# An S4 kernel generator: the fine magnitudes straight from the exponential, one product of 512 in place of one of 1024

## The chip, the cores and the metric

The kernel runs on one core of a Trainium2 chip. Its time is the device time of one execution in microseconds; smaller is better. Five engines run side by side, each with its own queue that it works off in order: PE (TensorE, matrix products), DVE (VectorE, elementwise), ACT (ScalarE, functions from tables, copies), POOL (GpSimd) and SP (SyncE, which here issues most transfers).

## The reference

A block of a network with two halves, over a sequence of 2048 positions and 512 channels. The first half is a diagonal state-space layer (S4): each channel has 128 complex states, and its convolution kernel K is a sum of 128 complex exponentials. The second half is a dense layer of 512 to 1792, Mish, and 1792 to 512. Cut to what matters:

```python
dt = exp(log_dt)[:, None]
logdA = dt * (A_re + 1j * A_im)             # 512 channels x 128 states
dB = dt * (B_re + 1j * B_im)
P = exp(logdA[:, :, None] * arange(2048))   # a power for each position
K = einsum("dn,dnl,dn->dl", C, P, dB).real  # 512 x 2048
y = irfft(rfft(pad(h)) * rfft(pad(K)))[:2048] + h * Dskip   # h: normalised, modulated input
x = x + ga * y
h = layernorm(x) * (1 + cb) + sb
x = x + gb * (mish(h @ w1 + b1) @ w2)
```

The diff concerns the generation of P and K.

## The kernel before, in words

A position l is written as 64 i + j, with i from 0 to 31 (coarse steps) and j from 0 to 63 (fine steps). The power at l is the product of a coarse power, exp(64 i logdA), and a fine one, exp(j logdA), which also carries the constant of the state (B, C and dt). So K for a channel is a product of two matrices over the 128 states: 32 coarse columns on one side, 64 fine columns on the other, once for the real parts and once for the imaginary ones. PE makes these products (`s_kgen`, L347, tile pkg).

The 512 channels go in 32 steps k of 16 channels. A coarse or fine power is a magnitude (a real exponential) times a cosine or a sine, and these come in two ways:

- **Angles.** PE makes the angles of 32 coarse and 32 fine columns (`s_ang`, L312, tile pang), ACT takes the absolute value and two sines (`s_sin`, L321) into a tile ec of 2 x 16 x 96 numbers a partition, with columns 0 to 31 coarse, 64 to 95 fine and 32 to 63 free. Only 32 fine angles are made, symmetric about the middle: the other 32 fine columns have the same angles with the sign turned, so the same cosines and the sines negated.
- **Magnitudes.** PE multiplies the logarithms of the magnitudes by constants (`mc`, made at L61 and L66), NM = 48 numbers a channel: 32 coarse steps, 8 steps of eight fine positions, 8 single fine positions. ACT takes the exponential of the product (`coarse`, L302, tiles pco and co), in two halves of 8 channels, so 384 numbers a partition and instruction. For the fine magnitudes, DVE multiplies the 8 by the 8 to 64 (`s_mag`, L329, tile m, 1024 numbers).

`comb` (L335) is the work of DVE that puts both together, four multiplies: the lower half of the fine columns (read from columns 95 down to 64, written to 32 to 63), the upper half's first plane, the same for the second plane with the sign turned, and the coarse columns. Then PE can make pkg. ACT copies it to SBUF (`s_ks`, L356, tile ks); DVE adds the direct term Dskip to four of its columns (`s_skip`, L360); PE transforms the coarse axis (`s_ka`, L363, tile pka), and ACT copies that to the large tile gk (`s_tm`, L371).

**The order.** The sines and the exponentials are in different tables of ACT, so the exponentials of 8 steps are made together in a `visit` (L581): table change, 16 pairs of product and exponential through two PSUM buffers, table change back. Visit 0 stands ahead of step 0, visits 1 to 3 behind steps 7, 15 and 23. The order of DVE, ACT and PE is written out by hand and forced. In step k, PE does pkg(k-1), pang(k+3), pka(k-3) and then other work; ACT does ks(k-1), other work, the sines of k+2 and the copy for k-3; DVE does `own`, the list made of comb(k), s_mag(k+1) and s_skip(k-2), with further work of the step spread between its entries (`extra`): parameters of later channels (`params`), the input's layer norm (`u_stats`, `u_norm`). Some of that other work on PE and ACT is the transform of the normalised input (`u_mm`, tile pua, and `u_out`); its result goes to memory. At the end of steps 7, 15 and 23, s_mag(k+1) comes behind the visit instead.

The tile ec has three buffers, so the sines of step k+3 need pkg(k) done; pang's PSUM has two buffers; co has nine and m two. Behind the generation stands the convolution itself in the frequency domain (`product`, `inverse`), and then the second half with its dense products (`mm1`, `mm2`).

## Time and profile before

| | us |
|---|---|
| median of three runs | 737.81 (733.92 to 740.18) |
| profiled execution | 739.76 |
| its span, first to last instruction | 738.0 |
| busy: PE, DVE, ACT | 644.8, 430.2, 317.6 |
| generation, with its start | 0 to about 276 |
| convolution and the dense half's start | about 276 to 390 |
| dense half | about 390 to 738 |

In the profile, a tile is named without its buffer's number, and groups of instructions by what they write and read: `ec<-ec,m` is a multiply of comb, `ec<-ec,co` its last one, `m<-co` is s_mag, `co<-pco` the exponential, `ks<-ks,dtap` is s_skip. Nearly all instructions go through a helper, so their lines are those of the helper (L119, L141, L147). A number in brackets behind an instruction is the time its engine sat idle before it, with what ended that. The granted clock is the share of its full clock that PE was given.

### The profile page before, as it was taken

The numbers are of one execution on the slowest core, as the hardware profiler recorded it, in microseconds if no ns is written. First come the engines' busy times: TensorE is split into PE (matmuls) and PEld (weight loads), VectorE is DVE, ScalarE is ACT, GpSimd is POOL, SyncE is SP. The second block draws the span as 40 slices with busy tenths as digits, with TensorE's granted clock in tenths as the row PEclk, the third lists the DMA queues.
The fourth block names the chain that finished last, engine by engine and source line by source line (L and its number), as shares of the span: only waits on it lengthen the run. The fifth ranks groups of instructions, "written<-read, shape, count | busy, mean of one in ns | idle before, by whom it ended". The sixth has DMA issues, their size and how long they took to land.

```text
span 738.0 us, 11828 instructions
## 1 busy us (share of the span) xinstructions
PE 644.8 (87%) x4848; PEld 438.9 (59%) x4848; DVE 430.2 (58%) x813; ACT 317.6 (43%) x466; POOL 5.0 (1%) x12
## 2 busy tenths in 40 slices
PE   0388889769889988999826999999999999999996
PEld 0246647546655752333205877887788877888884
DVE  8789989998978756876539224431424424441113
ACT  2466587677876953453305322322123222322220
POOL 2000000000000000000000000000000000000000
PEclk9969868997985999999976999999999999999998
DMA  6741023522323258996286522022400500011002
GB/s 184 270 147 49 30 81 107 187 87 80 137 87 115 88 172 239 301 298 205 85 204 183 127 58 57 1 50 64 104 11 1 115 0 1 1 34 25 0 1 57
DMA packets 34314, 74.56 MB, mean 101 GB/s; under 512 B 5418, under 2 KB 9902, under 8 KB 33748
## 3 DMA queue, kind: packets, MB, share of 16 engines
q1 hardware_dynamic: 33380, 72.17, 33.6%
q10 hardware_dynamic: 576, 1.05, 0.7%
q8 instruction: 38, 0.62, 0.3%
q0 software_dynamic: 304, 0.59, 0.3%
q14 instruction: 16, 0.13, 0.1%
HBM read 49.66 MB, written 24.13 MB: 100 GB/s over the span
## 4 chain that ended last, share of the span: by engine, by line
PE 72%; DVE 15%; ACT 6%; DMA 4%; issue 2%; SPq 0%; DVEq 0%; ACTq 0%
PE pm L798 22%; PE po L815 21%; PE pang L147 5%; DVE ec L119 4%; PE pub L147 4%; PE pz L147 4%; PE pkb L147 3%; PE pkg L147 3%; PE pka L147 3%; PE pco L147 3%; PE pua L147 2%; PE pia L763 2%; DVE raw L119 2%; DVE m L119 2%; ACT ec L141 1%
## 5 line engine op out<-in xcount | busy, mean ns | idle before, releaser
L798 PE MATMUL pm<-hh,w1h 128*128 128x512 f32 x448 | 143.3, 400 | 0.6 <-ACT hh L119 0.6
L141 ACT ACTIVATE mh<-pm,b 128x512 f32<-128x512 f32 x56 | 38.5, 688 | 229.3 <-PE pm L798 229.3
L119 DVE TENSOR_TENSOR mal<-mh,mah 128x512 fp32r<-128x512 f32 x56 | 38.7, 691 | 156.4 <-ACT mah L119 156.0
L798 PEld LDWEIGHTS pm<-hh,w1h 128*128 128x128 f32 x448 | 85.3, 190 | 21.8 <-ACT hh L119 1.5
L815 PE MATMUL po<-w2h,mah 128*128 128x512 f32 x224 | 89.5, 400 | 0.0
L798 PE MATMUL pm<-hh,w1l 128*128 128x512 f32 x224 | 89.3, 399 | 0.0
L815 PE MATMUL po<-w2l,mah 128*128 128x512 f32 x224 | 88.6, 396 | 0.0
L815 PE MATMUL po<-w2h,mal 128*128 128x512 f32 x224 | 88.6, 395 | 0.0
L147 PE MATMUL pang<-ac,s 96*128 96x512 f32 x128 | 55.1, 476 | 26.8 <-DMA s<-pkd 26.8
L119 DVE TENSOR_TENSOR ec<-ec,m 128x1024 f32<-128x1024 f32 x64 | 61.0, 954 | 9.1 <-ACT ec L141 8.6
L147 PEld LDWEIGHTS pkg<-ec 128*32 128x32 f32 x2048 | 36.2, 117 | 35.6 <-issue 29.5
L147 PE MATMUL pkg<-ec 128*32 128x64 f32 x2048 | 41.1, 236 | 14.3 <-DVE ec L119 11.5
L119 DVE TENSOR_TENSOR y<-pkb,f 128x1024 f32<-128x1024 f32 x32 | 37.7, 1220 | 25.3 <-PE pkb L147 25.3
L815 PEld LDWEIGHTS po<-w2h,mah 128*128 128x128 f32 x224 | 42.2, 188 | 14.6 <-ACT mah L119 4.9
L147 PEld LDWEIGHTS pang<-ac,s 96*128 96x128 f32 x128 | 28.6, 224 | 34.3 <-issue 27.6
L147 PE MATMUL pco<-mc,s 64*128 64x384 f32 x64 | 33.6, 603 | 17.6 <-ACT co L141 17.2
L798 PEld LDWEIGHTS pm<-hh,w1l 128*128 128x128 f32 x224 | 42.7, 191 | 10.1
L815 PEld LDWEIGHTS po<-w2h,mal 128*128 128x128 f32 x224 | 42.1, 188 | 10.1
L815 PEld LDWEIGHTS po<-w2l,mah 128*128 128x128 f32 x224 | 42.1, 188 | 9.7
L147 PE MATMUL pang<-am,s 96*128 96x512 f32 x128 | 44.9, 437 | 0.0
L119 DVE TENSOR_TENSOR m<-co 128x1024 f32<-128x1024 f32 x32 | 39.0, 1219 | 8.5 <-ACT co L141 8.5
L119 DVE TENSOR_TENSOR ec<-ec,co 128x1024 f32<-128x1024 f32 x32 | 39.1, 1221 | 0.0
(97 smaller groups left out, 867.8 us busy)
## 6 DMA issues: line engine op xcount, KB each, us to landing
ud<-u SPq DMA_DIRECT2D x16, 512.0 KB, 3.1
ur<-ud SPq DMA_DIRECT2D x32, 256.0 KB, 4.5
zd<-z SPq DMA_DIRECT2D x16, 512.0 KB, 2.9
zl<-zd SPq DMA_DIRECT2D x28, 256.0 KB, 4.9
x<-in_A_u SPq DMA_DIRECT2D x32, 128.0 KB, 2.9
x<-in_A_u SPq DMA_DIRECT2D x8, 512.0 KB, 6.7
out<-ot SPq DMA_DIRECT2D x32, 128.0 KB, 2.2
w1s<-in_B_w SPq DMA_DIRECT2D x8, 448.0 KB, 6.8
```

The source lines that it names most:

```text
L119: ins = getattr(self.engine, name)(*a, **kw)
L141: follow("act", nc.scalar.activation(out, in_, f, **kw))
L147: follow("pe", T.matmul(out, lhsT, rhs, start=start, stop=stop))
L763: T.matmul(p[64 * tl:64 * tl + 64, :], di, ZL[tt, hv][:, j % 2, tl, :], start=True, stop=True)
L798: T.matmul(p, w1[wi][:, k, fs], hh[:, hi, k, :], start=(n == 0), stop=(n == 3 * KB - 1))
L815: T.matmul(PO[tt][q], a[ai][:, P * q:P * q + P], w2[wi][:, f, :], start=(f == 0 and n == 0), stop=(f == FB - 1 and n == 2))
```

## The change

NM goes from 48 to 64: the constants are now one column for the factor 32, 31 coarse steps (1 to 31; step 0 has magnitude 1), and all of the first 32 fine steps, with the state's constant in these. So the coarse products and their exponentials grow from 384 to 512 columns. s_mag multiplies the 32 fine magnitudes by that of 32 steps, 512 numbers, to get the upper half; m has one buffer instead of two. comb's first multiply reads the lower magnitudes from co; its last one leaves column 0 out (31 columns of 32). In `own`, s_skip moves from the end to behind the first multiply, and s_mag from there to the end. The tile gs (gains of the input's modulation) moves to a pool that is closed at step 26.

```diff
-NM = 48
+NM = 64
...
-    fac = np.concatenate([64 * np.arange(32), 8 * np.arange(8), np.arange(8)])
+    fac = np.concatenate([[32], 64 * np.arange(1, 32), np.arange(32)])
...
-            mc[4 * d + part, d] = fac if part < 2 else np.arange(NM) < 32
+            mc[4 * d + part, d] = fac if part < 2 else np.arange(NM) >= 32
...
     def s_mag(k):
-        m = M2[k] = gen.tile([P, 16, 64], F32, tag="m2", name=f"m2_{k}", bufs=2)
-        V.tensor_mul(m.rearrange("p d (a b) -> p d a b", a=8),
-                     CO[k][:, :, 32:40, None].to_broadcast([P, 16, 8, 8]),
-                     CO[k][:, :, None, 40:48].to_broadcast([P, 16, 8, 8]))
+        M2[k] = gen.tile([P, 16, 32], F32, tag="m2", name=f"m2_{k}", bufs=1)
+        V.tensor_mul(M2[k], CO[k][:, :, 32:64], CO[k][:, :, 0:1].to_broadcast([P, 16, 32]))
 
     def comb(k):
         ec, m = EC[k], M2[k]
         v = Later()
-        v.tensor_mul(ec[:, :, :, 32:64], ec[:, :, :, 95:63:-1], m[:, None, :, 0:32].to_broadcast([P, 2, 16, 32]))
-        v.tensor_mul(ec[:, 0, :, 64:96], ec[:, 0, :, 64:96], m[:, :, 32:64])
-        v.scalar_tensor_tensor(ec[:, 1, :, 64:96], ec[:, 1, :, 64:96], -1.0, m[:, :, 32:64],
-                               op0=OP.mult, op1=OP.mult)
-        v.tensor_mul(ec[:, :, :, 0:32], ec[:, :, :, 0:32], CO[k][:, None, :, 0:32].to_broadcast([P, 2, 16, 32]))
+        v.tensor_mul(ec[:, :, :, 32:64], ec[:, :, :, 95:63:-1], CO[k][:, None, :, 32:64].to_broadcast([P, 2, 16, 32]))
+        v.tensor_mul(ec[:, 0, :, 64:96], ec[:, 0, :, 64:96], m)
+        v.scalar_tensor_tensor(ec[:, 1, :, 64:96], ec[:, 1, :, 64:96], -1.0, m, op0=OP.mult, op1=OP.mult)
+        v.tensor_mul(ec[:, :, :, 1:32], ec[:, :, :, 1:32], CO[k][:, None, :, 1:32].to_broadcast([P, 2, 16, 31]))
         return v.ops
...
-        g = conv.tile([P, 2, D], F32, name="gs")
+        g = pre.tile([P, 2, D], F32, name="gs")
...
         own = comb(k) if 0 < k < NG else []
+        own.insert(1, lambda: step(s_skip, k - 2))
         if k % 8 != 7:
-            own.insert(1, lambda: step(s_mag, k + 1))
-        own.append(lambda: step(s_skip, k - 2))
+            own.append(lambda: step(s_mag, k + 1))
```

## The prediction

> **What bounds the kernel now.** I read the page first, then busy times by stage, the groups of VectorE (DVE) and ScalarE (ACT), and last the order of time around the waits. The page's clock row:

> ```profile
> PEclk9969868997985999999976999999999999999998
> ```

> One slice is 18.5 us. Nearly all dips (to 5 to 8 tenths) lie between 20 and 276 us, where the kernel is generated: 32 steps k, and four visits in which ACT changes tables and makes the coarse exponentials. The diff's instructions all lie there. By stage (columns: us, then busy PE, PEld, DVE, ACT, POOL, then granted clock; after visit 0, the rows of 11 us hold the visits):

> ```profile
> 43.00:97.00 54.00, 47.19 (x642) 32.55 (x641) 52.25 (x92) 35.57 (x51) 0.00 (x0) 0.83 0.22 75
> 97.00:108.00 11.00, 9.36 (x45) 4.66 (x47) 8.75 (x19) 9.00 (x18) 0.00 (x0) 0.59 0.00 0
> 108.00:161.00 53.00, 44.72 (x711) 31.60 (x702) 51.46 (x102) 38.01 (x57) 0.00 (x0) 0.89 0.43 141
> 161.00:172.00 11.00, 9.12 (x72) 5.10 (x76) 10.23 (x13) 9.27 (x18) 0.00 (x0) 0.63 0.00 0
> 172.00:220.00 48.00, 43.32 (x683) 30.02 (x674) 41.06 (x70) 36.83 (x54) 0.00 (x0) 0.91 0.35 117
> 220.00:231.00 11.00, 8.63 (x69) 5.21 (x73) 9.31 (x11) 8.51 (x18) 0.00 (x0) 0.59 0.05 7
> 231.00:276.00 45.00, 43.06 (x796) 29.48 (x790) 29.05 (x40) 31.03 (x46) 0.00 (x0) 0.91 0.44 146
> ```

> DVE is full in the first two groups of steps (52.25 of 54, 51.46 of 53), has some air in the third (41.06 of 48) and much in the last (29.05 of 45), where PE is full (43.06). In the visits the clock is near half. So DVE time saved counts in two and a half groups of four, and PE and ACT time added counts in the visits and after them.

> **The change part by part.** DVE's groups up to 276 us, costliest first (behind the bar: busy us, mean ns of one, then idle time ahead of them):

> ```profile
> L119 DVE TENSOR_TENSOR ec<-ec,m 128x1024 f32<-128x1024 f32 x32 | 39.1, 1223 | 9.0 <-ACT ec L141 8.6
> L119 DVE TENSOR_TENSOR ec<-ec,co 128x1024 f32<-128x1024 f32 x32 | 39.1, 1221 | 0.0
> L119 DVE TENSOR_TENSOR m<-co 128x1024 f32<-128x1024 f32 x32 | 39.0, 1219 | 8.5 <-ACT co L141 8.5
> L119 DVE SCALAR_TENSOR_TENSOR ec<-ec,m 128x512 f32<-128x512 f32 x32 | 22.0, 686 | 0.0
> L119 DVE TENSOR_TENSOR ec<-ec,m 128x512 f32<-128x512 f32 x32 | 21.9, 685 | 0.2
> ```

> s_mag's product shrinks from 1024 to 512 elements: 1219 to 685 ns, 0.534 us less, by the row of that size. The last multiply of comb goes from 1024 to 992: the slope between 685 and 1219 is 1.04 ns an element, so 0.033 less; its rows of 31 that start one element in have no row here, so I bound them between that gain and, at the row's own price, nothing. Together 0.57 us a step, 18.2 us over 32. The first multiply only reads the magnitudes from another tile: same size, nothing.

> The visits. ACT's rows for 384 and for 512 elements out of PSUM, and one pair of coarse products on PE, with the pair of exponentials that follows it on ACT:

> ```profile
> L141 ACT ACTIVATE co<-pco 128x384 f32<-128x384 f32 x64 | 29.4, 489 | 8.9 <-PE pco L147 6.4
> L119 ACT COPY gk<-pka 128x512 f32<-128x512 f32 x32 | 19.4, 607 | 11.4 <-PE pka L147 11.3
> ```

> ```profile
> 223.51 1.07 PE L147 MATMUL pco<-mc,s 64*128 64x384 f32 x2 [0.19 <-ACT co L141]
> 224.78 1.07 PE L147 MATMUL pco<-mc,s 64*128 64x384 f32 x2 [0.19 <-ACT co L141]
> ```

> ```profile
> 224.24 0.88 ACT L141 ACTIVATE co<-pco 128x384 f32<-128x384 f32 x2 [0.38 <-PE pco L147]
> ```

> ```profile
> 232.06 1.06 PE L147 MATMUL pang<-am,s 96*128 96x512 f32 x2
> 232.90 1.06 PE L147 MATMUL pang<-ac,s 96*128 96x512 f32 x2
> ```

> A pair takes 1.27 us (223.51 to 224.78), and both engines wait in it: the two PSUM buffers make each half a ring, product, exponential, product. Both legs get longer: the exponential by 607 - 489 = 0.118 us, the product by 128 columns, which at this clock cost 0.84 / 2 x 128 / 512 = 0.105 (232.06 to 232.90 is two products of 512). So 0.22 a pair, 1.7 us for the 8 pairs of a visit. Bounds: nothing, if ACT's 0.38 of idle time took it up, and 0.45 a pair (3.6 a visit), if both halves stood in line; I take 1.7, since both waits show in every pair.

> The order. s_skip(k-2) moves from the end of DVE's step to behind its first multiply, s_mag from there to the end. For PE this is a gain once in each DVE-bound stretch: comb(k) is complete 1219 - 162 (a small row's price, the ks add) = about 1.1 us earlier inside its step. For DVE it is a new wait: s_skip(k-2) needs ACT's copy ks(k-2), and behind it queue the step's other three multiplies, for which the PE product pkg(k) waits. Where that copy stands behind a visit, DVE will stop. The rows:

> ```profile
> 57.56 0.37 ACT L119 COPY ks<-pkg 128x256 f32<-128x256 f32 x1 [3.53 <-PE pkg L147]
> ```

> ```profile
> 172.53 0.37 ACT L119 COPY ks<-pkg 128x256 f32<-128x256 f32 x1 [0.15 <-PE pkg L147]
> ```

> ```profile
> 58.42 1.22 DVE L119 TENSOR_TENSOR ec<-ec,m 128x1024 f32<-128x1024 f32 x1
> ...
> 128.07 0.29 DVE L119 SCALAR_TENSOR_TENSOR raw<-raw 128x128 f32<-128x128 f32 x1 [0.74 <-ACT raw L141]
> ...
> 168.66 1.22 DVE L119 TENSOR_TENSOR ec<-ec,m 128x1024 f32<-128x1024 f32 x1
> ...
> 182.73 1.23 DVE L119 TENSOR_TENSOR ec<-ec,m 128x1024 f32<-128x1024 f32 x1 [1.96 <-ACT ec L141]
> ```

> ```profile
> 77.34 1.15 PE L147 MATMUL pkg<-ec 128*32 128x64 f32 x64 [2.45 <-DVE ec L119]
> ...
> 132.52 1.16 PE L147 MATMUL pkg<-ec 128*32 128x64 f32 x64 [1.53 <-DVE ec L119]
> ...
> 154.54 1.15 PE L147 MATMUL pkg<-ec 128*32 128x64 f32 x64 [2.46 <-DVE rstd L119]
> ...
> 199.91 1.16 PE L147 MATMUL pkg<-ec 128*32 128x64 f32 x64 [2.89 <-DVE ec L119]
> ```

> ```profile
> 201.06 3.37 PE pang L147 x8
> ...
> 208.35 1.10 PE pkg L147 x60
> 209.45 2.00 PE pang L147 x8
> ```

> Group 0 (to visit 1). ks(0) comes 1.7 later, at 59.3, and ends at 59.6. DVE would open step 2 at 58.42 - 3 x 0.534 - 2 x 0.033 = 56.75, run 1.5 (its first multiply and one small add that is woven in) and stop 1.4 us for it. So of 1.7 saved, little is left; with step 2's own rest, step 3 opens 0.9 earlier. Step 3 saves 0.57, and comb(4) ends 1.1 earlier in its step: pkg(4), which starts at 77.34, starts 2.6 earlier. From there to visit 1 PE has no gap, so the visit comes 2.6 earlier.

> The clock there. After PE's 2.89 us gap ahead of 199.91 the eight pang products take 3.37, a step later 2.00: the clock fell, and pkg to pkg is 8.4 us (199.91 to 208.35). At full clock PE's step would be some 5.0 (8.4 x 2.00 / 3.37), and DVE would set the pace: its five multiplies and the small add, 5.2 by their rows, less 0.57, with one multiply of 512 that is woven in, 5.4. A lost clock costs about 3.0 (an estimate). [...] Yet behind 2.46 (154.54) the clock held: the ninth slice of the page's row, in which it lies, shows 9. With comb ending 1.1 earlier, PE's gap ahead of 77.34 falls to 1.9, as pkg(3) moves by 2.0 and pkg(4) by 2.6. Between nothing and 3.0 I add 1.0, since the gaps don't settle it. Group 0: 3.6 (2.6 to 5.6).

> Group 1 (visit 1 to 2). At 128.07 DVE waits for an arctangent that ACT runs behind the visit's work: 1.7 later. From there to pkg(14) at 154.54 DVE had no wait: steps 11 to 13 save 0.57 each, step 14 1.1, in sum 2.8. Net 1.1.

> Group 2 (visit 2 to 3). ks(15) moves from 172.53 to 174.2, while DVE, at step 17 from 168.66 less two products (1.1), has done its first multiply at 168.7: a stop of near 6 us. It is covered as far as it goes: before, DVE came to 182.73 with 1.96 of idle time, and the step there waits for ACT and PE, which are 1.7 late on their own. Then DVE leads again for a step and a half, 0.57 + 1.1: pkg(20) at 199.91 comes at the same distance from the visit, 0.0. But its gap shrinks from 2.89 to 1.2, under the 1.53 (132.52, in the eighth slice, also 9); I take the 3.0. Group 2: 3.0 (0 to 3.0).

> Group 3: PE-bound, visit 3 costs its 1.7. Nothing later changes: the tiles only lie elsewhere, the gains gs are dead at step 23, three steps before the tables that take their place load, and mc's extra 64 KB comes in before the first coarse product.

> Sum: 3.6 + 1.1 + 3.0 - 1.7 = 6.0 (2.0 to 8.0 with the bounds above). The profiled execution took 739.76 (span 738.0, so 1.76 around it): 733.8 for such a one. The median is 1.95 lower: 731.8; own range 729.8 to 735.8.

> **Rivals.** First, the denser visits keep the clock up. A product of 512 then takes 0.21 in place of 0.42, 1.7 us in the 8 pairs of a visit, and its weight loads shrink too, so some 2; and the slow step after visits 1 and 3 goes from 8.4 to 5.0. Three visits of 2 and two steps of 3.4 give 12.8 more than the forecast's 6.0: 719, call it 720. Against it: in 97 to 108 PE was busy 9.36 of 11 and the clock still 0.59. [...] 0.13.

> Second, nothing comes: the clock falls in the same places, and DVE's 0.57 a step becomes DVE idle time at ACT and PE, as it would in the third and fourth group anyway. Gain 0 to 2: 736 to 738. For it: PE at 47.19 of 54 in group 0. 0.25.

> Third, slower: s_skip's early place. Stops of 1.4 (step 2), about as much in step 9, 6 each in steps 17 and 25: 14.8 us, and visits 4 x 1.7 = 6.8, against 18.2 saved: 3.4 slower, 741; with one clock fall more, 744. It decides from where DVE has no idle time left to take the stops, that is, if the 1.96 at 182.73 and its like at step 26 vanish. Against it: in those steps DVE must wait for the late sines whatever it does before. 0.10.

> **How the numbers follow.** Forecast 0.52, rivals 0.13, 0.25, 0.10. 1% (7.4 us, about what a measurement of this kernel tells from no change; its three runs spread over 6.3) needs a gain that only the forecast's top and the first rival reach: 0.22 + 0.13 = 0.35 faster. Slower by over 1% takes the third rival with clock falls added: 0.06. The rest, 0.59, is within. The range leaves out the far end of the first rival and of the third: 724 to 740.

> **What would show it.** The product m at 685 ns and the last multiply near 1190; pairs in the visits at 1.48; pkg(4) 2.6 earlier; s_skip as a DVE wait for ACT ks of about 1.4, 1.4, 6 and 6 us behind the four visits; clock at full where now the third group has slow pang products. It is wrong if DVE's stops push pkg of steps 17 and 25, or if m with its broadcast doesn't halve.

## The result, and the profile after

The changed kernel takes 732.58 us in the median of 7 runs (729.82 to 735.84); the kernel before took 740.69 in its 7 (733.92 to 742.54). The ratio is 0.9927, 95% interval 0.9899 to 0.9955, so 3 to 7.5 us faster, 1% at most. (The two medians lie 8.1 us apart, the ratio makes 5.4 of it; the text goes by the ratio and its interval.) The forecast was 731.8, 6.0 us faster, with "within 1%" as the likeliest case. The profiled execution took 735.84 us (span 734.1) against 739.76.

Where the gain arises is read from ACT's timeline: the table change that opens visits 1 to 3, and PE's first product of the convolution, at which the generation is over. Before:

```profile
96.81 1.28 ACT L144 ACT_TABLE_LOAD   x1
...
160.45 1.28 ACT L144 ACT_TABLE_LOAD   x1
...
219.39 1.28 ACT L144 ACT_TABLE_LOAD   x1
```

```profile
276.05 3.65 PE L147 MATMUL pkb<-gk,mf 128*64 128x512 f32 x16 [1.16 <-ACT f L119]
```

After:

```profile
94.36 1.28 ACT L144 ACT_TABLE_LOAD   x1
...
157.45 1.28 ACT L144 ACT_TABLE_LOAD   x1
...
214.09 1.28 ACT L144 ACT_TABLE_LOAD   x1
```

```profile
272.42 3.65 PE L147 MATMUL pkb<-gk,mf 128*64 128x512 f32 x16 [1.16 <-ACT f L119]
```

The lead over the kernel before is 2.45 us at visit 1, 3.00 at visit 2, 5.30 at visit 3 and 3.63 at the end. So the four groups gave 2.45, 0.55, 2.30 and -1.67; behind the generation another 0.3 us is gained (the spans differ by 3.9).

The same stages of the changed kernel (busy PE, PEld, DVE, ACT, POOL, then the clock). The windows have the same edges, but the visits now begin up to 5 us earlier and reach over their ends:

```profile
43.00:97.00 54.00, 47.04 (x645) 31.70 (x644) 48.25 (x94) 39.40 (x55) 0.00 (x0) 0.85 0.22 75
97.00:108.00 11.00, 9.80 (x75) 5.10 (x77) 10.44 (x30) 8.46 (x17) 0.00 (x0) 0.50 0.00 1
108.00:161.00 53.00, 47.56 (x683) 31.91 (x673) 47.09 (x93) 40.26 (x59) 0.00 (x0) 0.85 0.43 140
```

DVE, which was full in groups 0 and 1 (52.25 of 54, 51.46 of 53), now has 5.8 and 5.9 us of air there. Its work shrank, but the stage shrank by much less. DVE's groups:

```profile
L119 DVE TENSOR_TENSOR ec<-ec,co 128x1024 f32<-128x1024 f32 x32 | 39.0, 1219 | 1.8 <-ACT ec L141 1.8
L119 DVE TENSOR_TENSOR ec<-ec,co 128x992 f32<-128x992 f32 x32 | 37.9, 1184 | 0.0
L119 DVE TENSOR_TENSOR m<-co 128x512 f32<-128x512 f32 x32 | 21.9, 684 | 6.0 <-ACT co L141 6.0
```

The product m is 684 ns (from 1219), the rows of 31 take 1184 (from 1221): their odd start costs nothing. A pair of the visits, PE first, then ACT:

```profile
218.99 1.28 PE L147 MATMUL pco<-mc,s 64*128 64x512 f32 x2 [0.20 <-ACT co L141]
220.47 1.28 PE L147 MATMUL pco<-mc,s 64*128 64x512 f32 x2 [0.20 <-ACT co L141]
```

```profile
219.82 1.09 ACT L141 ACTIVATE co<-pco 128x512 f32<-128x512 f32 x2 [0.39 <-PE pco L147]
```

A pair takes 1.48 us in place of 1.27, and both engines still wait for each other, by the same 0.20 and 0.39. And DVE's stops for s_skip, with the arctangent's wait among them:

```profile
60.51 0.17 DVE L119 TENSOR_TENSOR ks<-ks,dtap 128x4 f32<-128x4 f32 x1 [2.19 <-ACT ks L119]
...
109.35 0.17 DVE L119 TENSOR_TENSOR ks<-ks,dtap 128x4 f32<-128x4 f32 x1 [1.57 <-ACT ks L119]
...
127.42 0.29 DVE L119 SCALAR_TENSOR_TENSOR raw<-raw 128x128 f32<-128x128 f32 x1 [3.14 <-ACT raw L141]
...
171.84 0.17 DVE L119 TENSOR_TENSOR ks<-ks,dtap 128x4 f32<-128x4 f32 x1 [5.98 <-ACT ks L119]
...
228.58 0.17 DVE L119 TENSOR_TENSOR ks<-ks,dtap 128x4 f32<-128x4 f32 x1 [6.08 <-ACT ks L119]
...
237.03 0.17 DVE L119 TENSOR_TENSOR ks<-ks,dtap 128x4 f32<-128x4 f32 x1 [4.24 <-ACT ks L119]
...
267.02 0.17 DVE L119 TENSOR_TENSOR ks<-ks,dtap 128x4 f32<-128x4 f32 x1 [3.67 <-ACT ks L119]
```

They stand behind the four visits as forecast (1.4, 1.4, 6 and 6; the first is 2.19), with two more, of 4.24 and of 3.67 at the generation's end, that were not foreseen. The question for the experiments: which of the change's three parts (narrower product, longer visits, other order) gives and takes how much, and whether these stops cost anything.

### The profile page after: what moved, and what is told of

Its sections match the earlier page's. It is cut to its first block, busy times and chain, and to the rows that moved or that the text cites. A ratio compares the mean times of both kernels' runs of the same rounds, so it can differ in the third digit from the quotient of the medians.

```text
span 734.1 us, 11767 instructions
## 1 busy us (share of the span) xinstructions
PE 648.6 (88%) x4848; PEld 437.5 (60%) x4848; DVE 412.4 (56%) x813; ACT 323.7 (44%) x466; POOL 5.0 (1%) x12
## 4 chain that ended last, share of the span: by engine, by line
PE 50%; DVE 3%; DMA 2%; issue 0%; ACT 0%; SPq 0%; DVEq 0%; ACTq 0%
PE pm L795 22%; PE po L812 21%; PE pz L147 2%; PE pia L760 2%; PE pub L147 2%; PE pkb L147 1%; DMA zl<-zd 1%; PE pln L780 1%; DVE ot L119 1%; DVE y L119 0%; DVE w2l L119 0%; DMA zd<-z 0%; DVE x L119 0%; DMA out<-ot 0%; DVE rsq L119 0%
## 5 line engine op out<-in xcount | busy, mean ns | idle before, releaser
L141 ACT ACTIVATE mh<-pm,b 128x512 f32<-128x512 f32 x56 | 38.6, 689 | 229.7 <-PE pm L795 229.7
L119 DVE TENSOR_TENSOR mal<-mh,mah 128x512 fp32r<-128x512 f32 x56 | 38.7, 691 | 156.8 <-ACT mah L119 156.4
L147 PE MATMUL pang<-ac,s 96*128 96x512 f32 x128 | 55.0, 476 | 27.2 <-DMA s<-pkd 27.2
L119 DVE TENSOR_TENSOR ec<-ec,co 128x1024 f32<-128x1024 f32 x64 | 76.9, 1201 | 1.8 <-ACT ec L141 1.8
L147 PE MATMUL pco<-mc,s 64*128 64x512 f32 x64 | 39.8, 708 | 17.1 <-ACT co L141 17.1
L119 DVE TENSOR_TENSOR y<-pkb,f 128x1024 f32<-128x1024 f32 x32 | 37.7, 1219 | 25.1 <-PE pkb L147 25.1
L147 PEld LDWEIGHTS pkg<-ec 128*32 128x32 f32 x2048 | 34.9, 114 | 28.2 <-issue 18.9
L147 PEld LDWEIGHTS pang<-ac,s 96*128 96x128 f32 x128 | 28.6, 224 | 34.7 <-issue 27.6
L147 PE MATMUL pkg<-ec 128*32 128x64 f32 x2048 | 39.6, 230 | 7.1 <-DVE ec L119 5.3
L147 PE MATMUL pang<-am,s 96*128 96x512 f32 x128 | 45.3, 441 | 0.0
L147 PEld LDWEIGHTS pco<-mc,s 64*128 64x128 f32 x64 | 16.9, 269 | 38.9 <-ACT co L141 38.0
L141 ACT ACTIVATE co<-pco 128x512 f32<-128x512 f32 x64 | 35.5, 595 | 10.2 <-PE pco L147 9.5
```

Source lines behind the costliest of these rows:

```text
L119: ins = getattr(self.engine, name)(*a, **kw)
L141: follow("act", nc.scalar.activation(out, in_, f, **kw))
L147: follow("pe", T.matmul(out, lhsT, rhs, start=start, stop=stop))
```

## The experiments

Ratios are to the kernel before, run on the same chip; 1% is 7.4 us. The experiments ran on three chips, so where two ratios are set against each other, the chips can differ.

**Undo one part: s_skip back at the end.**

```diff
-        own.insert(1, lambda: step(s_skip, k - 2))
         if k % 8 != 7:
             own.append(lambda: step(s_mag, k + 1))
+        own.append(lambda: step(s_skip, k - 2))
```

> The changed kernel with s_skip back at the end of DVE's step, everything else kept. Theory (the stops of s_skip behind the visits are covered, except in group 0): DVE's waits for ACT ks of 6.0, 6.1 and 4.2 us vanish and are replaced by waits for the sines; only the 2.2 us at step 2 can come back, so 0 to 3 us faster than the changed kernel, ratio to the kernel before 0.989 to 0.994. Rival (s_skip's early place costs what its waits show, 24.7 us in all): at least 8 us faster, ratio under 0.983.

Measured: 733.12 us, 0.9945 (0.9925 to 0.9964), the changed kernel's time within the intervals. DVE's waits up to 276 us, of the changed kernel (first fence; us in total, times, longest) and of this one (second):

```profile
DVE ks L119 <- ACT ks L119: 24.7, 8, 6.1
```

```profile
DVE ec L119 <- ACT ec L141: 14.3, 7, 3.7
DVE ks L119 <- ACT ks L119: 9.9, 6, 3.7
```

The long waits for ks go, and waits for the sines stand in their place; DVE waits nearly as long in sum (24.2 us of these two kinds, against 24.7 and 1.8), and visit 1 opens at 93.98 in place of 94.36. The stops were covered, at step 2 nearly so. The rival falls.

**One part alone: the new order in the kernel before.** s_skip second, s_mag last, all else as before.

```diff
         own = comb(k) if 0 < k < NG else []
+        own.insert(1, lambda: step(s_skip, k - 2))
         if k % 8 != 7:
-            own.insert(1, lambda: step(s_mag, k + 1))
-        own.append(lambda: step(s_skip, k - 2))
+            own.append(lambda: step(s_mag, k + 1))
```

> The kernel before with the new order only: s_skip second, s_mag last; magnitudes, visits and m as before. Theory (the gain comes from the 18 us of DVE work removed): no gain, ratio 0.997 to 1.005, with stops of s_skip behind the visits. Rival (comb complete 1.1 us earlier in its step is what shortens the path): ratio 0.993 or less, as the whole change.

Measured: 733.40 us, 0.9961 (0.9935 to 0.9988). So the order brings some 3 us (1 to 5 by the interval) with no DVE work removed: by its middle value more than the theory allowed and less than the rival asked. This split it further.

**Halves of the order.** On the kernel before: s_mag at the end of the step with s_skip still behind it, and, the other way, only s_skip second.

```diff
# first
-            own.insert(1, lambda: step(s_mag, k + 1))
+            own.append(lambda: step(s_mag, k + 1))
# second
-        own.append(lambda: step(s_skip, k - 2))
+        own.insert(1, lambda: step(s_skip, k - 2))
```

> The kernel before with s_mag at the end of DVE's step, ahead of s_skip, which stays behind it; nothing else. Theory (the order's part of the gain is that comb is complete earlier in its step): the same as the new order alone, ratio 0.994 to 0.998. Rival (s_skip's place brings it, since pka can start earlier): ratio 0.999 to 1.002.

> The kernel before with s_skip behind the first multiply and s_mag still ahead of the other three; nothing else. Theory (s_skip's place by itself neither brings nor costs): ratio 0.998 to 1.003. Rival (its place brings the order's part of the gain): ratio 0.994 to 0.998; third possibility (its stops cost): over 1.004.

Measured: s_mag last 733.70 us, 0.9935 (0.9908 to 0.9961); s_skip second 739.66 us, 1.0016 (0.9977 to 1.0055). The order's gain is s_mag's place, 3 to 5 us. PE waits for comb, and what stands in front of comb's last three multiplies delays it: comb(4) takes 6.0 us from its first multiply to the end of its last in the kernel before, 5.0 with s_mag last, 6.75 with s_skip second. That this is how the time is gained fits, but is argued: PE's waits for comb are no shorter in sum (12.5 us in 9 waits with s_mag last, 11.5 in 5 before), and the granted clock was a little higher with s_mag last (0.930 in the mean of its runs, 0.926 before; with the whole new order 0.927 in both kernels). s_skip's place does nothing that can be measured (the interval is 3 us either way), though its waits for ks (13.1 us, 4 times) are in the trace.

**The visits' length.** The changed kernel with 384 columns. This version leaves out the magnitudes of half the fine steps, so only its time counts.

```diff
-NM = 64
+NM = 48
...
-    fac = np.concatenate([[32], 64 * np.arange(1, 32), np.arange(32)])
+    fac = np.concatenate([[32], 64 * np.arange(1, 32), np.arange(16)])
...
-        V.tensor_mul(M2[k], CO[k][:, :, 32:64], ...
+        V.tensor_mul(M2[k], CO[k][:, :, 16:48], ...
...
-        v.tensor_mul(ec[:, :, :, 32:64], ..., CO[k][:, None, :, 32:64] ...
+        v.tensor_mul(ec[:, :, :, 32:64], ..., CO[k][:, None, :, 16:48] ...
```

> The changed kernel with products and exponentials of 384 columns, as before; comb and s_mag read 32 columns that are there, so the magnitudes of half the fine steps are left out and replaced by others of the same size. Theory (the longer visits are on the path, 1.7 each): pairs of 1.27 us, 5 to 7 us faster than the changed kernel, ratio 0.983 to 0.988. Rival (the visits' length is covered by DVE work): ratio 0.991 to 0.995.

Measured: 725.75 us, 0.9864 (0.9828 to 0.9901). Its visit 2 lasts 11.04 us from table change to table change; the changed kernel's lasts 12.65:

```profile
154.09 1.28 ACT L144 ACT_TABLE_LOAD   x1
...
165.13 1.28 ACT L144 ACT_TABLE_LOAD   x1
```

```profile
157.45 1.28 ACT L144 ACT_TABLE_LOAD   x1
...
170.10 1.28 ACT L144 ACT_TABLE_LOAD   x1
```

So the longer visits cost 0.9927 - 0.9864 = 0.6%, near 5 us, as the theory said (three visits of 1.7). Against the new order alone (0.9961), this kernel differs by the narrow product and the 31 columns: 1.0%, some 7 us from 18 us of DVE work. By these figures the change is 3 from the order, 7 from the narrow product, less 5 for the visits. Each ratio is known to 2 or 3 us either way, so each of these differences to some 3 us.

**Opening the ring.** The changed kernel with four PSUM banks in the visits.

```diff
-        p = psum.tile([P, 512], F32, tag="pu", name=f"pco{k}{h}")
+        p = psum.tile([P, 512], F32, tag="pb" if k % 2 else "pu", name=f"pco{k}{h}")
```

> The changed kernel with the visits' products alternating over four PSUM banks in place of two (odd steps take the banks of pkg and pka). Theory (each half is a ring of product and exponential through one bank, so both engines wait): the ring opens, a pair falls from 1.48 towards ACT's 1.1, some 2.5 us a visit; 6 to 10 us faster than the changed kernel, ratio 0.979 to 0.986. Rival (PE's weight load and product in line set the pair at this clock): a pair of 1.4, within 2 us of the changed kernel, ratio 0.990 to 0.995.

Measured: 721.18 us, 0.9787 (0.9763 to 0.9810), 10 us faster than the changed kernel and the best version of this study but for its two siblings below, which are equal to it. Its visit 1 on ACT, and the last 12 of that visit's products on PE:

```profile
94.01 7.95 ACT L141 ACTIVATE co<-pco 128x512 f32<-128x512 f32 x16
```

```profile
94.66 6.18 PE L147 MATMUL pco<-mc,s 64*128 64x512 f32 x12 [1.41 <-ACT co L141]
```

ACT runs its 16 exponentials without a gap, 0.99 us a pair where it was 1.48. A visit is 3.5 us shorter (9.25 in place of 12.76 for visit 0), and more than the forecast's 2.5 comes back, since the exponentials overlap here (16 in 7.95 us are 497 ns each, where one lasts 595 ns by the changed kernel's row).

**Four banks in the kernel before.** The same line there.

> The kernel before with the visits' products over four PSUM banks, nothing else. Theory (the ring of one bank per half set the visits in both kernels, and the narrow product is worth its DVE time beside that): a pair of two exponentials of 384 falls from 1.27 to some 0.88, 3 us a visit; 8 to 11 us faster than the kernel before, ratio 0.985 to 0.990, so the change would be worth 5 to 8 us on top of it (four banks with the change gave 0.979). Rival (with the ring open, the change's exponentials of 512 cost as much as its DVE time brings): the same time as four banks with the change, ratio 0.977 to 0.982.

Measured: 729.77 us, 0.9901 (0.9865 to 0.9937), at the edge of what the theory gave. Its exponentials take 6.24 us a visit:

```profile
96.86 6.24 ACT L141 ACTIVATE co<-pco 128x384 f32<-128x384 f32 x16
```

With the ring open on both sides the change is worth 0.9901 to 0.9787, 1.1% or 8 us, against 5 with the ring: the rival falls. The visits still grow by 1.7 us each (7.95 - 6.24), so this is again the narrow product and the order, less the visits; why it is 8 here isn't resolved, with intervals this wide.

**s_skip with short visits.** Four banks with s_skip last everywhere, and with s_skip last only in the two steps behind a visit.

```diff
# second
+        late = k % 8 in (1, 2)
+        if not late:
+            own.insert(1, lambda: step(s_skip, k - 2))
...
+        if late:
+            own.append(lambda: step(s_skip, k - 2))
```

> The changed kernel with four banks and s_skip back at the end of DVE's step. Theory (its stops are covered whatever the visits cost): the same as four banks alone within 2 us, ratio 0.977 to 0.982. Rival (with short visits ACT's and PE's lateness goes, and the stops come onto the path): 3 to 8 us faster than four banks alone, ratio 0.968 to 0.975.

> Four banks, and s_skip at the end of DVE's step only in the two steps behind each visit, second in all others. Theory: within 2 us of four banks alone, ratio 0.977 to 0.982. Rival (the stops behind the visits alone are on the path): 3 us or more faster, ratio under 0.975.

Measured: 721.62 us, 0.9770 (0.9748 to 0.9792), and 720.63 us, 0.9767 (0.9746 to 0.9787). Neither can be told from four banks alone. s_skip's place is free in this kernel too.

**The clock behind a gap.** Four banks, with PE's gap ahead of pkg(4) and pkg(12) filled by products that are made twice.

```diff
-        for e in range(2) if half is None else (half,):
+        for e in (0, 1, 0, 1) if k in (7, 15) else range(2):
```

> Four banks, and the eight pang products of k = 7 and k = 15 made twice, 1.8 us of PE work in the two places where PE waits 1.9 us for DVE (ahead of pkg(4) and pkg(12)) and where the clock fell behind it with four banks alone. Theory (PE's gap is what lets the clock fall): gaps of some 0.1 us, pang at 2.0 behind both, no change in time that one look can tell. Rival (the clock falls by its own time, whatever the gap): pang at 3 or more behind at least one of them.

Four banks alone, the step from pkg(4):

```profile
73.23 1.15 PE L147 MATMUL pkg<-ec 128*32 128x64 f32 x64 [1.87 <-DVE ec L119]
...
75.45 1.06 PE L147 MATMUL pang<-ac,s 96*128 96x512 f32 x2
76.31 1.05 PE L147 MATMUL pang<-am,s 96*128 96x512 f32 x2
```

With the gap filled, pkg(4) and the products behind it (first fence), and pkg(12) (second):

```profile
73.08 1.15 PE L147 MATMUL pkg<-ec 128*32 128x64 f32 x64
...
74.50 0.60 PE L147 MATMUL pang<-am,s 96*128 96x512 f32 x2
74.93 0.62 PE L147 MATMUL pang<-ac,s 96*128 96x512 f32 x2
```

```profile
130.95 1.15 PE L147 MATMUL pkg<-ec 128*32 128x64 f32 x64
...
132.38 0.60 PE L147 MATMUL pang<-am,s 96*128 96x512 f32 x2
```

Two products go by in 1.06 us behind the gap and in 0.62 without one. The clock held in both filled places. The one execution took 721.88 us, no change: visit 1 opens 2.1 us earlier than with four banks alone (90.61 against 92.72), but the convolution's first product only 0.4 (258.51 against 258.93). Two places alone prove little: of the 18 gaps of 1.6 to 2.0 us that are counted below, the clock held behind 12.

## Why the prediction was right

**The time.** 731.8 forecast, 732.58 measured; 6.0 us forecast between two profiled executions, 3.9 measured (735.84 against 739.76), 5.4 by the ratio. It holds in size. That the times agree within 1 us is luck: the forecast stands on a median of three runs, 737.81, and from the median of all seven, 740.69, it would have been 734.7. By part as follows; the first three groups each gave less than forecast.

**DVE's work.** m at 684 and the last multiply at 1184 came out as forecast. That 18 us of it shorten the path by much less was right; by the runs 7.

**The visits.** 0.22 a pair forecast, 0.21 measured (1.48 against 1.27). Group 3, where nothing but its visit counts: -1.7 forecast, -1.67 measured. And the reason given, a ring through one bank, is what the run with four banks bears out.

**Group 0: 3.6 forecast, 2.45 measured.** pkg(4) came 0.84 earlier, not 2.6:

```profile
76.50 1.16 PE L147 MATMUL pkg<-ec 128*32 128x64 f32 x64 [1.88 <-DVE ec L119]
...
138.00 1.15 PE L147 MATMUL pkg<-ec 128*32 128x64 f32 x64 [1.94 <-DVE ec L119]
...
197.51 1.15 PE L147 MATMUL pkg<-ec 128*32 128x64 f32 x64 [1.28 <-ACT ec L141]
```

The step that failed is "ks(0) comes 1.7 later, at 59.3, and ends at 59.6": ks(0) began at 60.03, and s_skip could start only at 60.51. Two things were left out: the visit itself began 0.4 later in this execution, and the low clock held longer behind it (17.07 us, to 54.22, in place of 13.65, to 51.24), which delayed pkg(0) by another 0.4. So step 3 opened at 65.29 as in the kernel before, not 0.9 earlier. Then it waited 0.68 for a transfer of the gains, which hangs on the same late PE work. The 0.84 at pkg(4) is the 1.1 by which comb now ends earlier in its step (6.03 us from its first multiply to its end before, 4.93 after), less 0.26.

The rest of the 2.45 is the clock's. It fell behind pkg(4) in both kernels, but came back after 3.41 us in place of 6.83, so that pkg(5) starts at 83.24 in place of 85.70. The stretch ahead of it, in the kernel before (first fence, clock 0.50) and after (second, 1.00):

```profile
81.95:85.37 3.42, 3.42 (x21) 2.08 (x20) 3.35 (x10) 0.59 (x1) 0.00 (x0) 0.50 0.00 0
```

```profile
81.52:84.93 3.41, 3.41 (x85) 2.32 (x82) 3.38 (x8) 1.06 (x3) 0.00 (x0) 1.00 0.00 0
```

The sum had 2.6 from DVE and 1.0 from the clock; it was 0.84 and 1.6, and that the second made up for part of the first is luck.

**Group 1: 1.1 forecast, 0.55 measured.** The arctangent came 1.8 later as said. But behind a gap of 1.94 us ahead of pkg(12) (138.00) the clock fell for 6.83 us, pkg(13) came 8.3 later (146.33), and PE, not DVE, set pkg(14). In the kernel before it fell in the same place, behind a gap of 2.56, but for 3.41 us only, and pkg(13) came 6.5 after pkg(12). The sum had taken this group's clock as given.

**Group 2: 3.0 forecast, 2.30 measured.** pkg(20) came 1.28 us behind PE's last work where 1.2 was forecast, and the clock held as it said (1.00 from 173.68 to 214.64): the lead goes from 2.40 at pkg(20) to 5.29 at pkg(21), 2.9 where 3.0 was forecast. The other 0.6 was lost ahead of pkg(20), where the sum had 0.0. Half of it is the visit, which cost 2.0 here and not 1.7 (the other half isn't traced): in both kernels it begins at the high clock, but before that lasted to 163.88, for three of its pairs (6 exponentials in 3.02 us), and after to 160.03, for two (4 in 2.46).

**The order.** "A gain once in each DVE-bound stretch" of 1.1 us was right in kind: the runs trace it to s_mag's place alone. As a part by itself it measured 3 to 5 us, where the sum had 1.1 in each of three groups. The stops for s_skip cost nothing that can be measured, as the sum had it for all but the one at step 2, which it charged with 1.4.

**The rivals.** The denser visits did not keep the clock: it is 0.50 in the window from 97 to 108. "Nothing comes" is outside the interval, though a part of its reason came true: in groups 0 and 1 the clock fell in the same places. "Slower, s_skip's early place" is refuted three times over (s_skip last in the changed kernel, with four banks, and second in the kernel before).

## What to carry to other kernels

When a helper engine's product is halved, look first at what stands in front of the instruction that the busy engine waits for: moving one multiply behind it here gave about as much as the whole change. A wait in the trace, even of 6 us, need cost nothing: DVE's for s_skip, 24.7 us in sum, cost nothing that could be measured (732.58 us with them, 733.12 with s_skip last). Undo a wait once before believing in it. And where two engines both show short waits in every round of a loop, count the buffers between them before shortening either: two more PSUM banks gave 10 us on top of the change, which itself gave 5 (and 7 us in the kernel before).

## What was not expected of the hardware

PE's clock behind short gaps. In the twelve profiles of this study, I took every gap of over 0.2 us ahead of a step's pkg and read the clock from the eight pang products behind it (2.0 us at full clock, 2.5 to 3.8 if some or all run slowly). Visits are left out, as there the clock is low already (0.52 to 0.60 in visits 1 to 3 of the changed kernel).

| PE's gap, us | gaps | clock fell behind it |
|---|---|---|
| under 1.6 | 51 | 0 |
| 1.6 to 2.0 | 18 | 6 |
| 2.0 to 3.0 | 25 | 13 |
| over 3.0 | 4 | 4 |

```profile
129.31:132.73 3.42, 1.48 (x67) 1.30 (x66) 3.42 (x6) 0.95 (x3) 0.00 (x0) 1.00 0.93 288
132.73:136.14 3.41, 3.41 (x10) 2.21 (x11) 3.41 (x6) 3.41 (x6) 0.00 (x0) 0.50 0.68 220
```

```profile
129.05:132.46 3.41, 1.69 (x67) 1.56 (x68) 3.41 (x5) 0.94 (x3) 0.00 (x0) 1.00 0.87 278
132.46:135.87 3.41, 3.41 (x27) 2.06 (x25) 3.41 (x6) 3.41 (x5) 0.00 (x0) 1.00 0.66 211
```

PE worked 1.48 us of the first stretch and 1.69 of the second; the clock fell behind the first (0.50) and held behind the second (1.00).

The fall behind pkg(20) cost 2.9 us by the lead that the changed kernel gained there, while without those in the two filled places the generation ended only 0.4 earlier. The spread of one kernel's runs (6 us in 7 runs) may be that of these falls. The runs fit: of 17 of the kernel before, the fastest had a mean clock of 0.934 (731.71 us), the slowest 0.921 (740.70). That the falls are the cause was not tested.

The second: PE was busy for most of 10 us on end in visits 1 to 3 of the changed kernel, 1.28 of every 1.48 us in visits 1 and 3 and by the profile without a break in visit 2, and the clock did not come up in any of them: it was 0.50 from 95.17 to 115.66, from 160.03 to 173.68 and from 214.64 to 235.12. It fell at 160.03, in visit 2, behind a stretch (from 156.62) that holds the table change and in which PE worked 0.63 us: it waited 3.03 us for the first exponentials.
